# Spectral layer and gated FFN on one core: the first transform stage as four 64x64 quarters, the third stage in halves through one PSUM bank, one instruction for both bias additions

## The chip, the core and the metric

The kernel runs on one core of a Trainium2 chip. The metric is the device time of one execution in microseconds (us). The core has TensorE (PE in the profile, with PEld for its weight loads), VectorE (DVE), ScalarE (ACT), GpSimd (POOL), and SyncE (SP), which here only issues DMAs. TensorE writes into PSUM, eight banks of 2 KB per partition; a bank holds 512 float32 values per partition.

## The reference, cut to what matters

```python
X = np.fft.rfft(x, axis=1)                       # x: 8 x 3136 x 256
Xr, Xi = X.real, X.imag
Yr = Xr @ w_r - Xi @ w_i + b_r                   # 256 x 256 mixing, complex
Yi = Xr @ w_i + Xi @ w_r + b_i
Y = softshrink(Yr, 0.01) + 1j * softshrink(Yi, 0.01)
y = np.fft.irfft(Y, n=3136, axis=1)
h = np.maximum(y @ w_in, 0)                      # 256 -> 1024
gate = sigmoid(conv3_along_seq(h, conv_w))
out = (h * gate) @ w_out                         # 1024 -> 256
```

A complex transform of length 3136 along the sequence, a 256x256 complex mix with bias and soft threshold, the inverse transform, and then a gated feed-forward layer.

## The kernel before, in words

The transform of length 3136 = 56 x 56 is done in two matmul stages each way, and everything up to the inverse's first half is one pipeline over 56 items: 8 batches `b` times 7 groups `g` of four frequencies.

- **Stage 1** (`stage1`, and `stage1_head` for batch 0): a DFT of length 56 over the slow index `n` for a block of four columns `j` (`JC = 4`). Two interleaved sequences (`h` = 0, 1, even and odd `n`) are done together: the weights `f1` are a 112x112 matrix with the 56x56 DFT table in it twice and zeros elsewhere. One block is two float32 matmuls of 112 rows by 512 columns into a single bank (`ps_s1`, one buffer), each followed by an ACT copy into `a1`; one DMA loads the block's `xr` from `x`, one DMA stores `a1` into the DRAM scratch `sc1`.
- **Stage 2** (`stage2`): reads `sc1` back in another layout (`load_a2`) and does the second DFT, eight float32 matmuls of 128 columns. The result is split into a rounded part `fh` and a rest `fl` (ACT and DVE).
- **Mix** (`mix`): 36 matmuls into three banks `ps_mx0..2` (Karatsuba: three real products for a complex one). DVE adds each of the two biases to the third product (`p1`, two instructions, line 309), adds the other two products (line 313, four instructions), then the soft threshold on ACT and DVE, and a split into `sh` and `sl`.
- **Stage 3** (`stage3`): twelve matmuls into two banks `ps_s3` (four outputs of 256 columns), one ACT copy into `z1`, one DMA to the scratch `sc2`.
- After this pipeline, **stage 4** finishes the inverse transform and `up`/`down` do the feed-forward layer (from about 550 us to the end).

In this first part the eight banks are: 1 `ps_s1`, 2 `ps_s2`, 3 `ps_mx`, 2 `ps_s3`.

The main loop over `it` emits stage 2 of item `it`, the mix of item `it-1`, stage 3 of item `it-3`, and one or two stage 1 blocks ahead (`min(it + AHEAD, NG + 2 + it + it // 2)`). A generator `later()` converts the feed-forward weights from 64-bit floats beside it; each `next(background)` is about one DVE instruction of that conversion: five per item early, then 2.2 on average. The code's order is only the start: a list scheduler orders each engine's queue, and `reuse_waits` pools and PSUM buffers set what waits for what. All DMAs are issued by SP in order. The first batch's blocks are loaded at once (`hx0..6`; the first in two DMAs) and go through `stage1_head`, which borrows the `ps_mx` banks and shares the copies between ACT and DVE.

A float32 matmul in this program appears in the trace as two MATMUL records, each with a weight load ahead of it: stage 1's 98 instructions at line 245 are 196 records. They are called passes below. `float32r` matmuls (mix, stage 3, feed-forward) are one record each.

Of the kernel before, what the change touches and what calls it, by code (L numbers as in the profile page):

```python
# [9 lines left out]
F32 = mybir.dt.float32  # L10
# [4 lines left out]
ALU = mybir.AluOpType  # L15
PSUM = bass.MemoryType.PSUM
DRAM = bass.MemoryType.DRAM

B, S, D, FF = 8, 3136, 256, 1024
R = 56  # L20
U = 28
SL = 57
SP = 64
H = 28
LAM = 0.01
UG = 4
NG = U // UG
JC = 4
P = 128
# [5 lines left out]
def _tables():  # L35
    n = np.arange(R)
    u = np.arange(U)

    f = np.zeros((R, 2, U))
# [3 lines left out]
    f[:, 1, 0] = np.where(n % 2 == 0, 1.0, -1.0)  # L43
    fwd1 = np.zeros((2, R, U, 2, 2))
    for h in range(2):
        fwd1[h, :, :, :, h] = f.transpose(0, 2, 1)

# [8 lines left out]
    for uu in range(U):  # L56
        for s in range(SL):
# [14 lines left out]
            elif s < R:  # L72
                k = uu + R * s
# [14 lines left out]
    return {  # L88
        "fwd1": fwd1.transpose(1, 0, 2, 3, 4).reshape(2 * R, 2 * R).astype(np.float32),
        "fwd2": fwd2.reshape(2 * R, U * 2 * SP).astype(np.float32),  # L90
# [6 lines left out]
def spectral_ffn_kernel(ctx: ExitStack, tc: tile.TileContext, x, w_r, w_i, b_r, b_i,  # L97
# [19 lines left out]
    with ExitStack() as ab:  # L117
# [6 lines left out]
        DB, XRB, SL_ENG = 1, 3, nc.gpsimd  # L124
        ps1 = ab.enter_context(tc.tile_pool(name="ps1", bufs=1, space=PSUM))
        ps2 = ab.enter_context(tc.tile_pool(name="ps2", bufs=2, space=PSUM))
        psm = ab.enter_context(tc.tile_pool(name="psm", bufs=1, space=PSUM))
        psa = ab.enter_context(tc.tile_pool(name="psa", bufs=1, space=PSUM))

        f1 = c1.tile([K1, P], F32, name="f1")[:, 0:K1]  # L130
        t2 = c1.tile([K1, U, K2], F32, name="t2")
# [97 lines left out]

        def load_x(pool, b, jc, parts=1, **kw):  # L230

            xr = pool.tile([K1, JC, D], F32, name="xr", **kw)
            xv = x[b].rearrange("(n j) d -> n j d", j=H)[:, jc * JC:(jc + 1) * JC, :]
            w = JC // parts
            for k in range(0, JC, w):
                ld = nc.sync.dma_start(xr[:, k:k + w, :], xv[:, k:k + w, :])
            return xr, ld

        def stage1(b, jc):

            xr, _ = load_x(s1p, b, jc, bufs=XRB)
            a1 = s1p.tile([K1, JC, D], F32, name="a1", bufs=2)
            for j in range(0, JC, 2):
                ps = ps1.tile([K1, 2, D], F32, name="ps_s1")
                nc.tensor.matmul(ps, f1, xr[:, j:j + 2, :], start=True, stop=True)  # L245
                nc.scalar.copy(a1[:, j:j + 2, :], ps)  # L246
            return nc.sync.dma_start(sc1[b][:, jc * JC:(jc + 1) * JC, :], a1)

        def stage1_head(xs, b=0):

            with tc.tile_pool(name="ha", bufs=1, reuse_waits="tile") as ha:
                for jc, xr in enumerate(xs):
                    a1 = ha.tile([K1, JC, D], F32, name=f"ha{jc}")
                    for j in range(0, JC, 2):
                        k = (jc * 2 + j // 2) % 4
                        if k < 3:
                            ps = psm.tile([K1, 2, D], F32, name="ps_s1h", tag=f"ps_mx{k}")
                        else:
                            ps = ps1.tile([K1, 2, D], F32, name="ps_s1")
                        nc.tensor.matmul(ps, f1, xr[:, j:j + 2, :], start=True, stop=True)  # L260
                        if j:
                            nc.vector.tensor_copy(a1[:, j:j + 2, :], ps)
                        else:
                            nc.scalar.copy(a1[:, j:j + 2, :], ps)
                    st = nc.sync.dma_start(sc1[b][:, jc * JC:(jc + 1) * JC, :], a1)
            return st
# [24 lines left out]
        def mix(xs):  # L291
# [15 lines left out]
            half = (slice(0, SP), slice(SP, K2))  # L307
            for c in range(2):
                nc.vector.tensor_tensor(p1[:, c], ps[2], bias[:, c], op=ALU.add)
            for c in range(2):  # L310
# [13 lines left out]
        def stage3(b, g, s):  # L324

            sh, sl, _ = s
            ps = psa.tile([K1, UG, D], F32, name="ps_s3")
            for k in range(UG):
                u = g * UG + k
                for n, (lt, rh) in enumerate(((i1_hi, sh), (i1_hi, sl), (i1_lo, sh))):  # L330
                    nc.tensor.matmul(ps[:, k, :], lt[:, u, :], rh[:, k, :], start=(n == 0), stop=(n == 2))  # L331
            z1 = io.tile([K1, UG, D], F32, name="z1", bufs=2)
            nc.scalar.copy(z1, ps)
            nc.sync.dma_start(sc2[b][:, g * UG:(g + 1) * UG, :], z1)
# [12 lines left out]
        with tc.tile_pool(name="hx", bufs=1, reuse_waits="tile") as hx:  # L347
            xh = []
            for p in range(NG):
                xr, ld = load_x(hx, 0, p, parts=2 if p == 0 else 1, tag=f"hx{p}")  # L350
                xh.append(xr)
            with tc.issue_after(ld.ins):
                load_t2(0)
                load_mix()
                load_bias()
                st = stage1_head(xh)
# [16 lines left out]
        for it in range(n_it + 3):  # L373
# [15 lines left out]
            if WP0 <= it < n_it:  # L389
                with tc.issue_after(ss[it - 1][2].ins):  # L390
                    for _ in range(5 if it < CW_IT else 2 + (it % 5 == 0)):
                        next(background, None)
# [148 lines left out]
```

## Time and profile before

| | |
|---|---|
| median of 3 runs | 1766.77 us (1766.06 to 1769.52) |
| the profiled execution | 1769.05 us, its span 1767.3 us |
| granted TensorE clock | 0.995 |
| PE busy | 1731.0 us (98%), 12096 matmul records |
| PE weight loads | 1621.6 us (92%) |
| DVE busy | 1524.3 us (86%) |
| ACT busy | 1229.1 us (70%) |
| POOL busy | 134.7 us (8%) |
| DMA | 164.63 MB, 30.9% of 16 engines' span |

The profile is of one execution; 1.75 us lie around its span, and it is 2.28 us above the median of the runs. Busy time of PE counts a matmul until its modelled end, and successive matmuls overlap, so the distance between the starts of two matmuls is what one costs, and not its duration. The "chain" is followed back from the last instruction to whatever released each step.

### The profile page before, as it was taken

Reading aid. Unit: us, or ns where it says so; the run is one execution under the profiler, and the core shown is the slowest. Engines: PE = TensorE matmul, PEld = TensorE weight load, DVE = VectorE, ACT = ScalarE, POOL = GpSimd, SP = SyncE. Lnnn points to the kernel's source line nnn. Section 1 sums busy time; section 2 is a strip of 40 time slices with the busy share of each in tenths; the row PEclk is TensorE's granted clock in tenths of the full one; section 3 lists DMA queues with packets and bytes.
Section 4 is the critical chain, followed back from the end, with each engine's and each line's share of the span. In section 5 each row is a group of like instructions: output and inputs, shape, how many; then the busy total and the mean of one; then the engine's idle time right before and its main releaser. Section 6 shows DMA issues by size and latency. Waiting matters only on the chain.

```text
span 1767.3 us, 29387 instructions
## 1 busy us (share of the span) xinstructions
PE 1731.0 (98%) x12096; PEld 1621.6 (92%) x12096; DVE 1524.3 (86%) x1820; ACT 1229.1 (70%) x1590; POOL 134.7 (8%) x60
## 2 busy tenths in 40 slices
PE   6899999999998999999999999999999999999999
PEld 2788888888998999999999999999999999999998
DVE  2899999998896988988888888888888888888887
ACT  2667777776665777777777777777777777777766
POOL 0122222222232000000000000000000000000000
PEclk8999999999999999999999999999999999999999
DMA  9777677677534110111111011111101111100001
GB/s 263 216 230 236 196 232 216 192 230 228 164 111 136 43 43 22 32 53 53 32 53 53 22 55 51 49 46 52 43 22 43 53 43 43 42 22 22 22 22 42
DMA packets 107382, 164.63 MB, mean 93 GB/s; under 512 B 8816, under 2 KB 86000, under 8 KB 107248
## 3 DMA queue, kind: packets, MB, share of 16 engines
q1 hardware_dynamic: 107248, 162.74, 30.9%
q8 instruction: 96, 1.57, 0.4%
q14 instruction: 38, 0.31, 0.1%
HBM read 85.65 MB, written 77.07 MB: 92 GB/s over the span
## 4 chain that ended last, share of the span: by engine, by line
PE 93%; DMA 3%; DVE 1%; ACT 1%; issue 0%; SPq 0%; ACTq 0%
PE acc L470 31%; PE ps_h L442 31%; PE ps_mx L304 12%; PE ps_s L423 5%; PE ps_s L280 5%; PE ps_s L331 4%; PE ps_s L245 4%; DMA i_raw<-in_inv_dram 2%; DMA z<-sc 1%; DMA sc<-ha 0%; DMA a<-sc 0%; DMA sc<-a 0%; ACT a L246 0%; DVE cw L212 0%; DVE yl L430 0%
## 5 line engine op out<-in xcount | busy, mean ns | idle before, releaser
L470 PE MATMUL acc<-wout,gh 128*128 128x256 f32 x3136 | 567.0, 280 | 0.0
L451 DVE SCALAR_TENSOR_TENSOR c<-h,cw,c 128x896 f32<-128x896 f32 x448 | 513.1, 1147 | 47.3 <-ACT c L449 46.3
L442 PE MATMUL ps_h<-yh,win 128*128 128x450 f32 x1792 | 551.0, 368 | 0.1
L470 PEld LDWEIGHTS acc<-wout,gh 128*128 128x128 f32 x3136 | 493.7, 188 | 6.5
L470 PE MATMUL acc<-wout,gl 128*128 128x256 f32 x1568 | 437.6, 281 | 0.0
L444 ACT ACTIVATE h<-ps_h 128x900 f32<-128x900 f32 x224 | 207.7, 927 | 254.8 <-PE ps_h L442 254.8
L442 PEld LDWEIGHTS ps_h<-yh,win 128*128 128x128 f32 x1792 | 338.7, 189 | 26.4 <-DVE yl L430 0.8
L442 PE MATMUL ps_h<-yl,win 128*128 128x450 f32 x896 | 329.2, 367 | 0.0
L470 PEld LDWEIGHTS acc<-wout,gl 128*128 128x128 f32 x1568 | 293.7, 188 | 0.1
L457 DVE TENSOR_TENSOR gl<-c,gh 128x896 fp32r<-128x896 f32 x224 | 243.1, 1089 | 53.6 <-ACT gh L456 50.1
L453 DVE TENSOR_TENSOR c<-h,c 128x896 f32<-128x896 f32 x224 | 243.6, 1088 | 46.9 <-ACT c L452 46.7
L456 ACT CAST gh<-c 128x896 fp32r<-128x896 f32 x224 | 209.8, 942 | 49.4 <-DVE c L453 49.4
L452 ACT ACTIVATE c<-c 128x896 f32<-128x896 f32 x224 | 213.3, 952 | 23.9 <-DVE c L451 21.0
L304 PE MATMUL ps_mx<-wmix_lo,fh 128*128 128x256 f32 x672 | 202.2, 301 | 0.0
L304 PE MATMUL ps_mx<-wmix_hi,fh 128*128 128x256 f32 x672 | 196.9, 294 | 0.5 <-DVE v L313 0.3
L304 PE MATMUL ps_mx<-wmix_hi,fl 128*128 128x256 f32 x672 | 188.7, 282 | 1.3 <-DVE fl L288 1.2
L442 PEld LDWEIGHTS ps_h<-yl,win 128*128 128x128 f32 x896 | 168.9, 189 | 11.0
L449 ACT ACTIVATE c<-h,cw 128x896 f32<-128x896 f32 x168 | 175.5, 1044 | 2.6 <-DVE gl L457 0.2
L321 POOL TENSOR_TENSOR sl<-v,sh 128x1024 fp32r<-128x1024 f32 x56 | 134.5, 2402 | 423.1 <-PE ps_s L331 300.0
L313 DVE TENSOR_TENSOR v<-ps_mx,p 64x512 f32<-64x512 f32 x224 | 154.0, 688 | 3.3
L304 PEld LDWEIGHTS ps_mx<-wmix_lo,fh 128*128 128x128 f32 x672 | 126.4, 188 | 12.3 <-issue 12.3
L304 PEld LDWEIGHTS ps_mx<-wmix_hi,fl 128*128 128x128 f32 x672 | 126.0, 188 | 11.8 <-issue 9.9
(84 smaller groups left out, 2023.0 us busy)
## 6 DMA issues: line engine op xcount, KB each, us to landing
a<-sc SPq DMA_DIRECT2D x56, 448.0 KB, 5.0
sc<-z SPq DMA_DIRECT2D x56, 448.0 KB, 3.3
z<-sc SPq DMA_DIRECT2D x56, 448.0 KB, 3.8
xr<-in_x_dram SPq DMA_DIRECT2D x55, 448.0 KB, 4.7
out_dram<-o SPq DMA_DIRECT2D x27, 896.0 KB, 4.0
sc<-a SPq DMA_DIRECT2D x49, 448.0 KB, 4.9
sc<-ha SPq DMA_DIRECT2D x7, 448.0 KB, 7.5
win_bits<-in_moe_w_in_dram SPq DMA_DIRECT2D x4, 512.0 KB, 7.6
```

What stands on the lines that cost most here:

```text
L304: nc.tensor.matmul(ps[c][:, k, :], lt, rh, start=(n == 0), stop=(n == len(mm) - 1))
L313: nc.vector.tensor_tensor(v[dst, :, k, :], ps[c][src], p1[src, c], op=ALU.add)
L321: SL_ENG.tensor_tensor(sl, v, sh.bitcast(F32), op=ALU.subtract)
L442: nc.tensor.matmul(ps[:, a, 0:CH + 2], lt, rh, start=(n == 0), stop=(n == len(mm) - 1))
L444: nc.scalar.activation(h, ps[:, :, 0:CH + 2], AF.Relu)
L449: nc.scalar.mul(c, h[:, :, 0:CH], cw[:, 0, f:f + 1])
L451: nc.vector.scalar_tensor_tensor(c, h[:, :, k:k + CH], cw[:, k, f:f + 1], c, op0=ALU.mult, op1=ALU.add)
L452: nc.scalar.activation(c, c, AF.Sigmoid)
L453: nc.vector.tensor_tensor(c, h[:, :, 1:CH + 1], c, op=ALU.mult)
L456: nc.scalar.copy(gh, c)
L457: nc.vector.tensor_tensor(gl, c, gh.bitcast(F32), op=ALU.subtract)
L470: nc.tensor.matmul(acc[m // 2][:, m % 2, :], lt[:, sl], rh[:, f, :], start=(f == 0 and n == 0 and m % 2 == 0), stop=(f == NF - 1 and n == ...
```

## The change

- `fwd1` becomes one 56x56 table, padded to 64x64 and placed twice, at partitions 0 and 64. `xr` has the even `n` on partitions 0 to 55 and the odd on 64 to 119, loaded by two DMAs.
- `quarters` does a block in four matmuls of 56 rows and 64 output columns, with 512 moving columns each: for each pair of columns `c` and each `h`, rows `h*64..`, output partitions `c*64..`, bank `ps[h]`. In the program these four carry an array tile of 64x64 at the four positions (0,0), (0,64), (64,0), (64,64).
- `ps1` has two buffers, one bank for each `h`. The ACT copies stay two of 512 columns, now on 128 partitions; the store is two DMAs, with runs of 2 KB where there were 4 KB.
- To free the bank, stage 3 uses one bank and goes in two halves, six matmuls and an ACT copy each.
- The bias sums `p1` are one DVE instruction of 1024 columns that reads the PSUM bank twice, where there were two of 512.
- The weight conversion beside the loop goes at 1.67 steps per item after the early ones, where it went at 2.2.
- The head's first block is not loaded by columns in two parts any more, and its copies and banks alternate by block.

```diff
...
-    fwd1 = np.zeros((2, R, U, 2, 2))
-    for h in range(2):
-        fwd1[h, :, :, :, h] = f.transpose(0, 2, 1)
+    fwd1 = np.zeros((2, SP, SP))
+    fwd1[:, :R, :R] = f.transpose(0, 2, 1).reshape(R, R)
...
-        ps1 = ab.enter_context(tc.tile_pool(name="ps1", bufs=1, space=PSUM))
+        ps1 = ab.enter_context(tc.tile_pool(name="ps1", bufs=2, space=PSUM))
...
-        f1 = c1.tile([K1, P], F32, name="f1")[:, 0:K1]
+        f1 = c1.tile([P, P], F32, name="f1")[:, 0:SP]
...
+            xr = pool.tile([P, JC, D], F32, name="xr", **kw)
+            xv = x[b].rearrange("(n h j) d -> h n j d", h=2, j=H)
+            for h in range(2):
+                ld = nc.sync.dma_start(xr[h * SP:h * SP + R], xv[h, :, jc * JC:(jc + 1) * JC, :])
...
+        def quarters(ps, xr):
+
+            for c in range(2):
+                for h in range(2):
+                    rows = slice(h * SP, h * SP + R)
+                    nc.tensor.matmul(ps[h][c * SP:(c + 1) * SP], f1[rows, :], xr[rows, 2 * c:2 * c + 2, :], start=True, stop=True)
+
+        def store_a1(b, jc, a1):
+
+            for c in range(2):
+                j = jc * JC + 2 * c
+                st = nc.sync.dma_start(sc1[b].rearrange("(w h) j d -> w h j d", h=2)[:, :, j:j + 2, :], a1[c * SP:c * SP + R])
+            return st
+
         def stage1(b, jc):
 
             xr, _ = load_x(s1p, b, jc, bufs=XRB)
-            a1 = s1p.tile([K1, JC, D], F32, name="a1", bufs=2)
-            for j in range(0, JC, 2):
-                ps = ps1.tile([K1, 2, D], F32, name="ps_s1")
-                nc.tensor.matmul(ps, f1, xr[:, j:j + 2, :], start=True, stop=True)
-                nc.scalar.copy(a1[:, j:j + 2, :], ps)
-            return nc.sync.dma_start(sc1[b][:, jc * JC:(jc + 1) * JC, :], a1)
+            a1 = s1p.tile([P, 2, JC // 2, D], F32, name="a1", bufs=2)
+            ps = [ps1.tile([P, JC // 2, D], F32, name="ps_s1") for h in range(2)]
+            quarters(ps, xr)
+            for h in range(2):
+                nc.scalar.copy(a1[:, h], ps[h])
+            return store_a1(b, jc, a1)
...
-            for c in range(2):
-                nc.vector.tensor_tensor(p1[:, c], ps[2], bias[:, c], op=ALU.add)
+            nc.vector.tensor_tensor(p1, ps[2].unsqueeze(1).broadcast_to([K2, 2, UG // 2, D]), bias, op=ALU.add)
...
-            ps = psa.tile([K1, UG, D], F32, name="ps_s3")
-            for k in range(UG):
-                u = g * UG + k
-                for n, (lt, rh) in enumerate(((i1_hi, sh), (i1_hi, sl), (i1_lo, sh))):
-                    nc.tensor.matmul(ps[:, k, :], lt[:, u, :], rh[:, k, :], start=(n == 0), stop=(n == 2))
             z1 = io.tile([K1, UG, D], F32, name="z1", bufs=2)
-            nc.scalar.copy(z1, ps)
+            for c in range(0, UG, 2):
+                ps = psa.tile([K1, 2, D], F32, name="ps_s3")
+                for k in range(2):
+                    u = g * UG + c + k
+                    for n, (lt, rh) in enumerate(((i1_hi, sh), (i1_hi, sl), (i1_lo, sh))):
+                        nc.tensor.matmul(ps[:, k, :], lt[:, u, :], rh[:, c + k, :], start=(n == 0), stop=(n == 2))
+                nc.scalar.copy(z1[:, c:c + 2, :], ps)
...
-                    for _ in range(5 if it < CW_IT else 2 + (it % 5 == 0)):
+                    for _ in range(5 if it < CW_IT else 1 + (it % 3 > 0)):
...
```

The scheduler also moves instructions. On TensorE, this is a round in the middle of the pipeline before, word for word from the program's order (`ps_s` with a number is a PSUM tile: line 331 writes stage 3's, 245 stage 1's, 280 stage 2's):

```order
L331 MATMUL ps_s_1382<-sl,i_hi 112x256
L331 MATMUL ps_s_1382<-sh,i_lo 112x256
L245 MATMUL ps_s_1401<-xr,f_113 112x512
L280 MATMUL ps_s_1420<-t_114,a_1195 128x128 x4
L280 MATMUL ps_s_1429<-t_114,a_1195 128x128 x4
L304 MATMUL ps_mx_1442<-wmix_hi,fh 128x256
...
L245 MATMUL ps_s_1404<-xr,f_113 112x512
```

Each stage 1 matmul stands alone between others, twice a round, and stage 3's twelve are together. The same part of a round of the changed program (line 242 is `quarters`, 340 stage 3, 288 stage 2, 312 the mix):

```order
L340 MATMUL ps_s_2252<-sh,i_lo 112x256
L312 MATMUL ps_mx_2313<-wmix_hi,fl 128x256
L242 MATMUL ps_s_2723<-xr,f_113 64x512
L312 MATMUL ps_mx_2311<-wmix_hi,fh 128x256
...
L340 MATMUL ps_s_2260<-sh,i_hi 112x256
...
L288 MATMUL ps_s_2402<-t_114,a_2173 128x128 x4
L288 MATMUL ps_s_2411<-t_114,a_2173 128x128 x4
L312 MATMUL ps_mx_2424<-wmix_hi,fh 128x256
L312 MATMUL ps_mx_2424<-wmix_lo,fh 128x256
L242 MATMUL ps_s_2724<-xr,f_113 64x512
L242 MATMUL ps_s_2723<-xr,f_113 64x512
L242 MATMUL ps_s_2724<-xr,f_113 64x512
```

The four quarters of a block (tiles 2723 and 2724, two each) are put apart: one, then 26 mix and six stage 3 matmuls and stage 2's eight, then three. Stage 3's second half (2260) stands 20 mix matmuls and a quarter behind the first (2252). Counted over the whole order, the 224 quarters lie in 84 runs with no other matmul inside: one run of 34 at the start, then 14 runs of four, 12 of three, 41 of two, 16 of one. Up to the fourth mix there are 52 quarters in 9 runs (before: 24 matmuls), from there 172 quarters in 75 runs (before: 88 matmuls). The last quarter stands after the 36th of 56 mixes, where the last stage 1 matmul before stood after the 46th.

On SP, the DMAs of a round before (line 334 stores `z1`, 270 loads `a2`, 236 loads `xr`, 247 stores `a1`):

```order
L334 DMA sc_1_66<-z_1940 112x1024
L270 DMA a_2065<-sc_2_59 112x4x256
L236 DMA xr<-in_x_dram 112x1024
L247 DMA sc_3_60<-a_1945 112x1024
L334 DMA sc_1_66<-z_2049 112x1024
```

and of one in the changed program (342, 278, 234, 248 in the same order):

```order
L342 DMA sc_2_67<-z_2588 112x1024
L234 DMA xr<-in_x_dram 56x1024 x2
L248 DMA sc_4_61<-a_3172 112x1x512 x2
L278 DMA a_2962<-sc_3_60 112x4x256
L342 DMA sc_2_67<-z_2701 112x1024
```

The loads of `xr` and the stores of `a1` are two issues each, of half the size; the order of the kinds is the same but for `a2`.

More of the change, by code (lines that the diff above doesn't have):

```diff
@@ L88, in _tables @@
     return {
-        "fwd1": fwd1.transpose(1, 0, 2, 3, 4).reshape(2 * R, 2 * R).astype(np.float32),
+        "fwd1": fwd1.reshape(2 * SP, SP).astype(np.float32),
         "fwd2": fwd2.reshape(2 * R, U * 2 * SP).astype(np.float32),
@@ L228, in later, with load_x @@
                     yield from split_weight(*asked.pop(0))
[L230 to L236, printed above, removed]
-            return xr, ld
+        def load_x(pool, b, jc, **kw):
+            xr = pool.tile([P, JC, D], F32, name="xr", **kw)
+            xv = x[b].rearrange("(n h j) d -> h n j d", h=2, j=H)
+            for h in range(2):
+                ld = nc.sync.dma_start(xr[h * SP:h * SP + R], xv[h, :, jc * JC:(jc + 1) * JC, :])
+            return xr, ld
+        def quarters(ps, xr):
[8 more added lines that the diff above has]
+            return st
         def stage1(b, jc):
             xr, _ = load_x(s1p, b, jc, bufs=XRB)
-            a1 = s1p.tile([K1, JC, D], F32, name="a1", bufs=2)
-            for j in range(0, JC, 2):
-                ps = ps1.tile([K1, 2, D], F32, name="ps_s1")
-                nc.tensor.matmul(ps, f1, xr[:, j:j + 2, :], start=True, stop=True)
-                nc.scalar.copy(a1[:, j:j + 2, :], ps)
-            return nc.sync.dma_start(sc1[b][:, jc * JC:(jc + 1) * JC, :], a1)
+            a1 = s1p.tile([P, 2, JC // 2, D], F32, name="a1", bufs=2)
[4 more added lines that the diff above has]
+            return store_a1(b, jc, a1)
         def stage1_head(xs, b=0):
@@ L252, in stage1_head @@
                 for jc, xr in enumerate(xs):
[L253 to L265, printed above, removed]
+                    a1 = ha.tile([P, 2, JC // 2, D], F32, name=f"ha{jc}")
+                    if jc % 2:
+                        ps = [psm.tile([P, JC // 2, D], F32, name="ps_s1h", tag=f"ps_mx{h}") for h in range(2)]
+                    else:
+                        ps = [ps1.tile([P, JC // 2, D], F32, name="ps_s1") for h in range(2)]
+                    quarters(ps, xr)
+                    nc.scalar.copy(a1[:, 0], ps[0])
+                    nc.vector.tensor_copy(a1[:, 1], ps[1])
+                    st = store_a1(b, jc, a1)
             return st
@@ L349, in spectral_ffn_kernel @@
             for p in range(NG):
-                xr, ld = load_x(hx, 0, p, parts=2 if p == 0 else 1, tag=f"hx{p}")
+                xr, ld = load_x(hx, 0, p, tag=f"hx{p}")
                 xh.append(xr)
```

## The prediction

> **What bounds the kernel now.** First the chain of waits on the page, then the busy time by windows, to find the stretch in which the changed stages run and what limits it.
>
> ```profile
> PE 93%; DMA 3%; DVE 1%; ACT 1%; issue 0%; SPq 0%; ACTq 0%
> ```
>
> ```profile
> core 0: us, PE busy (x) PEld busy (x) DVE busy (x) ACT busy (x) POOL busy (x), PEclk, DMA share, GB/s
> 0.00:25.00 25.00, 16.95 (x28) 5.87 (x28) 7.94 (x14) 7.04 (x12) 0.20 (x4) 1.00 0.90 264
> 25.00:50.00 25.00, 15.60 (x80) 11.88 (x81) 7.64 (x14) 7.67 (x16) 0.00 (x0) 0.73 0.97 238
> 50.00:75.00 25.00, 20.18 (x143) 17.13 (x143) 20.99 (x34) 13.70 (x24) 2.41 (x1) 1.00 0.93 261
> 75.00:100.00 25.00, 23.61 (x172) 20.55 (x170) 23.12 (x40) 16.70 (x31) 7.48 (x3) 1.00 0.52 150
> 100.00:120.00 20.00, 18.90 (x132) 16.04 (x133) 17.66 (x36) 13.69 (x23) 4.75 (x2) 1.00 0.90 265
> 160.00:250.00 90.00, 90.00 (x671) 80.09 (x670) 85.04 (x138) 65.42 (x104) 23.81 (x10) 1.00 0.77 227
> 480.00:550.00 70.00, 66.48 (x566) 65.87 (x565) 67.39 (x109) 47.20 (x69) 22.84 (x10) 0.99 0.38 112
> 600.00:1767.00 1167.00, 1162.96 (x7989) 1119.93 (x7988) 1011.57 (x1004) 836.14 (x977) 0.00 (x0) 1.00 0.13 40
> ```
>
> Up to 120 us PE is busy for 16.95 + 15.60 + 20.18 + 23.61 + 18.90 = 95.2 us of 120: 24.8 us of idle PE lie there, beside DMA engines at 0.90 to 0.97 in most of it. From 160 us PE never stops (90.00 of 90.00), while DVE has 85.04 and ACT 65.42 of the same 90. Behind 550 us the feed-forward layer runs, which the change doesn't touch. So what stage 1 costs is what it takes of PE, in the stretch in which PE is full.
>
> What one instruction costs on PE is read from the distance between starts, in the chain and in the timeline.
>
> ```profile
> 109.52 0.86 PE ps_s L245 x2
> 155.55 3.04 PE ps_mx L304 x26
> 164.69 3.04 PE ps_mx L304 x26
> ```
>
> ```profile
> 150.60 0.28 PE L331 MATMUL ps_s<-sh,i_lo 128*112 128x256 f32 x1
> 150.72 1.02 PE L245 MATMUL ps_s<-xr,f 112*112 112x512 f32 x2
> 151.58 1.95 PE L280 MATMUL ps_s<-t,a 112*128 112x128 f32 x16
> ```
>
> One stage 1 matmul holds PE for 0.86 us (150.72 to 151.58), as two records: a pass of 512 columns costs 0.43 us. A mix matmul costs 3.04 / 26 = 0.117 us. A round of the pipeline lasts 164.69 - 155.55 = 9.14 us, and its two stage 1 matmuls are 1.72 us of it.
>
> ```profile
> L245 PE MATMUL ps_s<-xr,f x196: 590/592/1167, 32.6 to 474.7; 112*112 112x512 f32 x196
> ```
>
> A pass's record lasts 0.592 us at the median, 0.16 us beyond the 0.43 after which the next one starts: results are still on their way out of the array while the next matmul already runs.
>
> **The change part by part.** *Quarters.* A block had two matmuls of two passes, 4 x 0.43 = 1.72 us. Now it has four matmuls of two passes each over 512 columns; nothing in the diff makes a pass shorter, since the columns that stream through are as many. So it is eight passes, and all depends on how many run at the same time on different quarters of the array, which no record of this kernel shows: every matmul here uses the full array. The bounds are 8 x 0.43 = 3.44 us (none at a time) and 0.86 us (all four).
>
> I take a value between, from the order. The timeline shows PE's matmuls starting in program order, and a quarter's second pass uses the same rows of the array as its first, so it can't start until the first has streamed, 0.43 us later. The next quarter stands behind that second pass. In an in-order queue its first pass can start beside it, but not earlier. So n quarters in a row take (n + 1) passes: a block in one piece 5 x 0.43 = 2.15 us, and in two pieces of two 6 x 0.43 = 2.58. Both are more than 1.72. The Trainium skill, TensorE: Matmul & The Clock Gate, "The mechanism", says that tiles of the array overlap, but that matmuls start and end strictly in the order of the program; the timeline agrees on the starts, and no run here shows tiles.
>
> From the fourth mix on, about where PE is full, the order has 172 quarters in 75 runs in place of 88 matmuls: (172 + 75) x 0.43 = 106.2 us in place of 88 x 0.86 = 75.7. That is **+30.5 us**.
>
> *Going in and out of quarters.* Each run begins and ends beside full-array matmuls. If the array must be empty before it is divided in another way, the 0.16 us by which records overlap is lost at each border: 75 x 2 x 0.16 = **+24.0 us**. The bounds are 0 (matmuls of different shapes, 112 and 128 rows, follow each other without a gap now) and 0.34 us a border, if the weight load of the next matmul isn't hidden either:
>
> ```profile
> L245 PEld LDWEIGHTS ps_s<-xr,f 112*112 112x112 f32 x196 | 29.0, 178 | 18.4 <-issue 11.4 <-ACT a L246 7.0
> L246 ACT COPY a<-ps_s 112x512 f32<-112x512 f32 x98 | 58.3, 595 | 19.7 <-PE ps_s L245 18.4 <-DMA sc<-a 0.4
> L333 ACT COPY z<-ps_s 112x1024 f32<-112x1024 f32 x56 | 56.7, 1013 | 78.8 <-PE ps_s L331 74.7 <-DMA sc<-a 4.0
> L309 DVE TENSOR_TENSOR p<-ps_mx,bias 128x512 f32<-128x512 f32 x112 | 71.8, 684 | 0.2
> L319 DVE SCALAR_TENSOR_TENSOR v<-v,r 128x1024 f32<-128x1024 f32 x56 | 70.1, 1251 | 16.7 <-ACT r L318 16.2
> ```
>
> (0.16 + 0.178 = 0.34, so up to 51 us). I take 0.16, since the load is hidden by the matmul ahead wherever PE is full now. The Trainium skill, TensorEngine Tiling (Array Packing), "Key Properties", has this rule: a change of the tiling mode, not of the tile alone, drains TensorE. It speaks against the change; the trace has no such border.
>
> *Up to the fourth mix* there are 52 quarters in 9 runs for 24 matmuls: 61 x 0.43 = 26.2 us for 20.6, and 18 borders x 0.16 = 2.9, so 8.5 us more of PE, beside 24.8 us of idle PE. Most of it is hidden by transfers that end later; I take **+2 us** (0 to 8.5).
>
> *Stage 3 in halves.* Two ACT copies of 512 columns (595 ns by line 246) for one of 1024 (1013 ns) are 0.18 us more of ACT in a round, where ACT has (90 - 65.42) / 90 x 9.14 = 2.5 us free: nothing. The new wait is that of the second half's first matmul for the copy of the first half; behind it on PE stand the mix matmuls, and for these DVE waits. In the order 20 mix matmuls lie between, 2.3 us, and ACT stood idle for 74.7 us in 56 rounds waiting for just this stage, so it takes the copy at once: 0. If a copy of 1.0 us (line 333's length) is ahead of it and only twelve mix matmuls (1.4 us) lie between, the wait is 1.0 + 0.6 - 1.4 = 0.2 us a round, 11 us in all: the other bound.
>
> *Bias in one instruction.* A DVE instruction of 1024 columns takes 1251 ns (line 319) and two of 512 take 1368: 0.12 us less of DVE a round. DVE isn't what the round waits for (85.04 of 90): 0. The same for the slower weight conversion, which only spreads DVE work over more rounds.
>
> *DMAs and SP.* Two issues more for each load and each store; on SP the next issues behind them are `z1` and `a2`.
>
> ```profile
> xr<-in_x_dram SPq DMA_DIRECT2D x55, 448.0 KB, 4.7
> sc<-a SPq DMA_DIRECT2D x49, 448.0 KB, 4.9
> ```
>
> They land within 5 us now, and a block is loaded rounds ahead: nothing in the full stretch, where the DMA share is 0.77. In the first 75 us shorter runs may cost or spare a microsecond or two: -2 to +3, I take 0.
>
> Sum: 30.5 + 24.0 + 2 = +56.5 us. The profiled execution took 1769.05 us, 2.28 above the median: 1825.5 there, **1823 us** as a median.
>
> **The rivals.**
>
> *No overlap at all*, so that the quarters do not do what their tiles say: 172 x 0.86 = 147.9 for 75.7 us, +72.2, with the borders +24.0, and the first run of 34 quarters (29.2 us for about 14.6 before) delays the first stores by some 8 us: +104, 1871 us. For it: nothing in the trace shows two matmuls side by side. Against it: the instructions have disjoint rows or columns and disjoint banks.
>
> *Full overlap within a run*, if each quarter has a queue of its own, so that the next quarter needn't wait for the second pass ahead. A run then takes 0.86 us whatever its length: 75 x 0.86 = 64.5 for 75.7, which is -11.2. With borders of 0.16 us it ends at -11.2 + 24.0 = +13, 1780 us. What limits the gain is in the order: only 14 runs hold four quarters, and a run of one or two costs as much.
>
> *Full overlap and free borders*, which is the other side: -11.2 us, about 1756 us. It decides as soon as a border costs less than 11.2 / 150 = 0.075 us. A round would then be shorter at the cost of DVE's slack, and DVE, at 85.04 / 90 x 9.14 = 8.6 us a round less the 0.12 of the bias, would be next; the rounds with quarters, (75 x 0.86) / 32 + 7.4 = 9.4 us (7.4 = 9.14 - 1.72; 32 rounds from the fourth mix to the 36th), stay above that, so DVE takes nothing back. For it: full-array matmuls of unlike shapes border without a gap today. Against it: a second pass would have to be overtaken. The Trainium skill, TensorEngine Tiling (Array Packing), "Key Properties", has tiles loading weights and multiplying in parallel, independently of each other; on that rule alone, this case would be the likeliest.
>
> **How the numbers follow.** The forecast with (n + 1) passes has 0.42; its own range goes from free borders (1769.05 - 2.28 + 30.5 = 1797) to borders of 0.34 us (1850). No overlap has 0.20, full overlap with borders 0.20, full overlap and free borders 0.18. A measurement of this kernel tells 0.2%, 3.5 us, from no change. Faster is the last case and a little of the one before it with small borders, 0.20; within 0.2% is only a border cost near 0.075 us, 0.06; slower the rest, 0.74. The range goes from 1754 to 1855: it holds all cases but no overlap.
>
> **What would show it.** In the profile after, the distance between the starts of line 242's records inside a run of four: eight records over five distances of 0.43 us if I am right, over two if all overlap, over eight if none do. At a border: the distance from the last quarter's start to the next full-array matmul, 0.43 us if it is free and 0.59 if the array empties. PE should stay full from 120 to about 500 us, with rounds of about 11.4 us ((106.2 + 24.0) / 32 + 7.4) up to the 36th mix and of 7.4 behind it, and line 340 should not wait for ACT. A round of 9.4 us or less, DVE as the engine waited for, or DMA waits at line 242 would prove me wrong.

## The result, and the profile after

The changed kernel takes **1832.38 us** (median of 4 runs, 1830.94 to 1834.84) beside 1768.14 us of the kernel before on the same chip (4 runs, 1766.06 to 1773.74): a ratio of **1.0353, 95% interval 1.0337 to 1.0369**. It is slower by 64 us. Its profiled execution took 1833.43 us, with a span of 1831.2.

First the chain of waits on the page of the changed kernel, by engine. Before, it read PE 93%, DMA 3%, DVE 1%.

```profile
PE 79%; DVE 13%; issue 4%; DMA 2%; ACT 1%; SPq 1%; POOL 0%; DVEq 0%; ACTq 0%
```

Then its busy time by windows, the stretches of before where they can be compared.

```profile
core 0: us, PE busy (x) PEld busy (x) DVE busy (x) ACT busy (x) POOL busy (x), PEclk, DMA share, GB/s
0.00:25.00 25.00, 12.98 (x44) 3.19 (x44) 4.66 (x9) 5.38 (x9) 0.21 (x4) 1.00 0.81 206
...
160.00:250.00 90.00, 85.66 (x623) 67.20 (x622) 78.09 (x104) 55.71 (x100) 21.84 (x9) 1.00 0.69 205
...
480.00:550.00 70.00, 63.07 (x521) 60.88 (x520) 69.20 (x104) 45.89 (x79) 19.71 (x8) 1.00 0.46 126
```

From 160 to 250 us PE was busy for 90.00 of 90; now it has 4.3 us of gaps, and DVE is less busy as well (78.09 for 85.04). Neither engine is full: they wait for each other. Within the pipeline, the chain by line (here from 120 to 500 us) goes through PE for less than half.

```profile
by line: PE ps_mx L312 21.0%; PE ps_s L242 11.6%; issue 11.2%; DVE v L320 8.2%; PE ps_s L288 7.4%; PE ps_s L340 7.1%; DVE fl L294 6.3%; DVE p L316 5.7%; DVE fl L296 4.4%; DVE v L326 2.4%; DVE d L293 2.4%; POOL sl L328 1.3%; DVE win_m L198 1
```

**Where the 64 us lie.** The start of the soft threshold on DVE (line 326; 319 before) marks each of the 56 items. Read off the timelines of the two profiled executions:

| start of the soft threshold of | item 4 | item 40 | item 55 |
|---|---|---|---|
| before | 98.6 us | 427.6 us | 550.2 us |
| after | 109.2 us | 492.5 us | 614.2 us |
| lost up to there | 10.6 | 64.9 | 64.0 |

So 10.6 us are lost in the head, 54.3 in the 36 rounds from item 4 to item 40 (383.3 / 36 = 10.65 us a round, for 329.0 / 36 = 9.14), and nothing behind them. The last quarter runs at 436.7 us; some 5 of the 54.3 us are lost behind it, between items 36 and 40 (59.6 us lost up to item 36).

**The quarters overlap.** This is PE's timeline of the changed kernel around a run of three quarters, with the mix matmuls on both sides.

```profile
213.12 0.28 PE L312 MATMUL ps_mx<-wmix_hi,fl 128*128 128x256 f32 x1
213.34 1.08 PE L242 MATMUL ps_s<-xr,f 56*64 56x512 f32 x6
214.35 0.38 PE L312 MATMUL ps_mx<-wmix_hi,fh 128*128 128x256 f32 x1
214.57 0.28 PE L312 MATMUL ps_mx<-wmix_lo,fh 128*128 128x256 f32 x1
```

Six passes that would take 6 x 0.43 = 2.6 us one behind another hold PE for 1.01 us (213.34 to 214.35). Shorter stretches of the same timeline part the six records: three start together, and three start together 0.47 us later.

```profile
213.34 0.65 PE L242 MATMUL ps_s<-xr,f 56*64 56x512 f32 x3
...
213.81 0.60 PE L242 MATMUL ps_s<-xr,f 56*64 56x512 f32 x3
```

The first passes of neighbours start 7 ns apart, and only then come the second passes. Runs of one, two, three and four quarters hold PE for 1.00, 1.01, 1.01 and 1.02 us at the median. The distances on both sides are stretched too: 0.22 us instead of 0.12 from the last mix matmul to the first quarter, and 0.22 from the first to the second mix matmul behind. From the last mix matmul ahead to the second behind it is 1.45 us, less two usual distances of 0.117: **a run costs 1.21 us**, whatever its length, where one full-array matmul cost 0.86. The border, in and out, is 0.35 us a run.

The Trainium skill, TensorEngine Tiling (Array Packing), "Key Properties", states that tiles work in parallel and that a change of mode drains TensorE; the trace agrees with the first. The longer distances on both sides fit the second, and 0.35 us is the price of two changes here; but the ends of matmuls are modelled, so the trace doesn't show whether the array is empty at a border.

**But PE is not all that the rounds wait for.** From item 4 to item 40 the idle time between PE's records grows from 2.1 to 18.6 us. Here is a run of four in the same kernel, 6 us earlier, and what comes behind it.

```profile
206.88 0.28 PE L312 MATMUL ps_mx<-wmix_lo,fh 128*128 128x256 f32 x1
207.08 1.09 PE L242 MATMUL ps_s<-xr,f 56*64 56x512 f32 x8
209.82 0.39 PE L312 MATMUL ps_mx<-wmix_hi,fl 128*128 128x256 f32 x1 [1.65 <-DVE fl L296]
```

PE stands still for 1.65 us behind the quarters, until DVE has written `fl`. DVE's and GpSimd's timeline of that moment:

```profile
205.18 1.21 DVE L326 SCALAR_TENSOR_TENSOR v<-v,r 128x1024 f32<-128x1024 f32 x1
206.32 2.85 DVE L198 TENSOR_TENSOR win_m<-win_m,win 128x512 f32<-128x512 f32 x1
209.09 0.68 DVE L296 TENSOR_TENSOR fl<-d,fh 128x512 fp32r<-128x512 f32 x1
209.69 0.68 DVE L199 TENSOR_TENSOR win<-win_m,win_rest 128x512 fp32r<-128x512 f32 x1
...
205.63 2.98 POOL L328 TENSOR_TENSOR sl<-v,sh 128x1024 fp32r<-128x1024 f32 x1 [7.96 <-PE ps_s L340]
```

Line 198 and line 199 are the same kind of instruction on tiles of the same size, and yet 2.85 us and 0.68. The long one lies under GpSimd's split `sl` (line 328, 205.63 to 208.61) and ends 0.56 us behind it (9.17 - 8.61): it did not run slowly, it waited. Behind it in DVE's order stands line 296, and for that PE waits. The same moment before:

```profile
204.18 0.69 DVE L199 TENSOR_TENSOR win_m<-win_m,win 128x512 f32<-128x512 f32 x1
204.78 0.69 DVE L288 TENSOR_TENSOR fl<-d,fh 128x512 fp32r<-128x512 f32 x1
205.39 2.81 DVE L313 TENSOR_TENSOR v<-ps_mx,p 64x512 f32<-64x512 f32 x4
...
205.73 2.37 POOL L321 TENSOR_TENSOR sl<-v,sh 128x1024 fp32r<-128x1024 f32 x1 [6.76 <-PE ps_s L331]
```

Here the split (205.73 to 208.10) lies under the four additions of line 313 (205.39 to 208.20), which read one operand from PSUM, and none of the four is longer for it (2.81 / 4 = 0.70 us). The line views of the changed kernel say the same over all items. Min, median and max in ns:

```profile
L320 DVE TENSOR_TENSOR v<-ps_mx,p x224: 667/689/696, 65.1 to 612.3; 64x512 f32<-64x512 f32 x112
...
L296 DVE TENSOR_TENSOR fl<-d,fh x56: 676/683/2872, 52.9 to 600.2; 128x512 fp32r<-128x512 f32 x56
```

Line 320 reads PSUM and never exceeds 696 ns, line 296 reads two tiles in SBUF and reaches 2872. Between 40 and 620 us of the timeline, DVE instructions that stand by themselves and are longer than 1.3 us number 5 before (5.5 us beyond their usual length) and **25 after (47 us)**, and all of the 25 lie under the split. The Trainium skill, SBUF — State Buffer, "SBUF: two separate sides", states that VectorE and GpSimd share a pair of SBUF ports as an exclusive lock, held for a whole instruction, which a VectorE instruction with two SBUF inputs takes too; the trace agrees, for the two kinds of instruction above.

What moved the split is in the waits. It writes `sl`, which has one buffer, so it waits until stage 3 of the item ahead has read the old `sl`. Of the kernel after, from 120 to 500 us: engine and line, what it waited for, us in total, times, longest:

```profile
POOL sl L328 <- PE ps_s L340: 270.5, 34, 10.5
DVE v L320 <- POOL sl L328: 34.3, 14, 3.2
ACT d L291 <- DVE fl L296: 22.2, 13, 2.9
```

The wait for stage 3 was there before, in the same window:

```profile
POOL sl L321 <- PE ps_s L331: 267.1, 40, 7.6
```

But stage 3 now ends later: its second half stands 20 mix matmuls and a quarter behind the first, as the order showed, and in the traces it starts 5.3 us behind it at the median of items 4 to 40, where it was 0.7. From the end of `sh` to the start of the split the median of these items went from 2.8 us to 8.8, out from under the PSUM additions. Since `v` has to live until the split has read it, line 320 now waits for GpSimd too: 34.3 us.

**The head.** SP's queue, first the kernel after and then before:

```profile
1.19 9.48 SPq L234 DMA_DIRECT2D xr<-in_x_dram  x14
...
13.61 0.39 SPq L152 DMA_DIRECT2D wm_raw<-in_w_i_dram  x1
...
19.48 14.14 SPq L248 DMA_DIRECT2D sc<-ha  x14
...
36.91 1.40 SPq L278 DMA_DIRECT2D a<-sc  x3
```

```profile
1.18 4.32 SPq L236 DMA_DIRECT2D xr<-in_x_dram  x8
...
8.42 0.38 SPq L153 DMA_DIRECT2D wm_raw<-in_w_i_dram  x1
...
16.80 7.76 SPq L265 DMA_DIRECT2D sc<-ha  x7
...
30.72 1.39 SPq L270 DMA_DIRECT2D a<-sc  x3
```

The first load of stage 2's input is issued 6.2 us later. All of DVE's copies of the head but the first stand behind the split of the mix weights (line 156) in its order, and that waits for the `w_i` load, issued 5.2 us later. Before, four of them ran ahead of that split, from 7.98 to 16.98 us.

```profile
9.97 0.69 DVE L272 COPY ha<-ps_s1h 128x512 f32<-128x512 f32 x1 [1.90 <-PE ps_s1h L242]
21.33 0.69 DVE L156 TENSOR_TENSOR wm<-wm_raw,wm_raw 128x512 f32<-128x512 f32 x1 [10.67 <-DMA wm_raw<-in_w_i_dram]
...
22.55 0.68 DVE L272 COPY ha<-ps_s 128x512 f32<-128x512 f32 x1
```

### The profile page after: what moved, and what is told of

Same layout as the page of the kernel before. It is cut to its first block, busy times and chain, and to the rows that moved or that the text cites. A ratio compares the mean times of both kernels' runs of the same rounds, so it can differ in the third digit from the quotient of the medians.

```text
span 1831.2 us, 29833 instructions
## 1 busy us (share of the span) xinstructions
PE 1767.7 (97%) x12320; PEld 1617.2 (88%) x12320; DVE 1561.4 (85%) x1764; ACT 1231.8 (67%) x1646; POOL 143.8 (8%) x60
## 4 chain that ended last, share of the span: by engine, by line
PE 79%; DVE 13%; issue 4%; DMA 2%; ACT 1%; SPq 1%; POOL 0%; DVEq 0%; ACTq 0%
PE ps_h L450 30%; PE acc L478 30%; PE ps_mx L312 6%; PE ps_s L431 5%; DVE v L320 3%; PE ps_s L242 3%; PE ps_s L288 3%; PE ps_s L340 2%; DVE fl L294 2%; DVE p L316 2%; DMA xr<-in_x_dram 1%; DVE fl L296 1%; DVE v L326 1%; DVE d L293 1%; DMA wm_raw<-in_w_i_dram 0%
## 5 line engine op out<-in xcount | busy, mean ns | idle before, releaser
L312 PE MATMUL ps_mx<-wmix_lo,fh 128*128 128x256 f32 x672 | 189.7, 282 | 0.0
L320 DVE TENSOR_TENSOR v<-ps_mx,p 64x512 f32<-64x512 f32 x224 | 153.9, 687 | 37.5 <-POOL sl L328 34.3
L328 POOL TENSOR_TENSOR sl<-v,sh 128x1024 fp32r<-128x1024 f32 x56 | 143.6, 2565 | 483.8 <-PE ps_s L340 316.3
L312 PEld LDWEIGHTS ps_mx<-wmix_hi,fh 128*128 128x128 f32 x672 | 128.8, 192 | 28.4 <-DVE v L320 7.5
```

The lines of the kernel that those rows point to most:

```text
L312: nc.tensor.matmul(ps[c][:, k, :], lt, rh, start=(n == 0), stop=(n == len(mm) - 1))
L320: nc.vector.tensor_tensor(v[dst, :, k, :], ps[c][src], p1[src, c], op=ALU.add)
L328: SL_ENG.tensor_tensor(sl, v, sh.bitcast(F32), op=ALU.subtract)
```

## The experiments

**Theory 1**: stage 3 in halves makes `sl` live longer; GpSimd's split starts later and falls on DVE instructions that read only SBUF, and these, with PE behind them, are the lost rounds. **Theory 2**: the rounds are lost to the quarters themselves, scattered in runs with a border each, and to what they made of the order. All ratios are to the kernel before, run on the same chip; medians of 4 or 5 runs.

| | ratio, 95% interval | item 4 | rounds 4 to 40 | long DVE instr. |
|---|---|---|---|---|
| before | 1 | 98.6 us | 9.14 us | 5 |
| after | 1.0353 (1.0337 to 1.0369) | 109.2 | 10.65 | 25 |
| split on VectorE | 1.0274 (1.0256 to 1.0291) | 110.6 | 9.93 | 0 |
| before + halves | 1.0262 (1.0247 to 1.0278) | 100.8 | 10.28 | 48 |
| after, `sl` in two tiles | 1.0110 (1.0093 to 1.0127) | 105.7 | 9.33 | 17 |
| after, two `sl` buffers | 1.0182 (1.0166 to 1.0197) | 108.9 | 9.47 | 20 |
| before + quarters | 1.0212 (1.0196 to 1.0229) | 105.5 | 9.91 | 6 |
| before + halves, `sl` in two tiles | 1.0038 (1.0024 to 1.0052) | 96.3 | 9.35 | 17 |

### The split on VectorE (e1)

```diff
-        DB, XRB, SL_ENG = 1, 3, nc.gpsimd
+        DB, XRB, SL_ENG = 1, 3, nc.vector
```

> The changed kernel, with the split sl = v - sh on VectorE in place of GpSimd. Theory 1 (what costs the time is GpSimd's split: 25 VectorE instructions that overlap it take 47 us more than usual, and line 320 waits 34 us for it): no VectorE instruction above 1.3 us is left, VectorE has 1.1 us more of its own in a round, and the time falls to 1775 to 1805 us. Theory 2 (the quarters put in 84 places and the new order cost the time, on TensorE): VectorE only gets more to do, 1835 to 1890 us.

1816.72 us. With nothing on GpSimd not one DVE instruction is longer than usual, and the kernel is 16 us faster than the change although DVE has 56 x 1.22 = 68 us more to do. But the time lies between the ranges of both theories. Its windows, DVE being the third pair of numbers:

```profile
160.00:250.00 90.00, 90.00 (x673) 72.06 (x672) 86.02 (x125) 60.84 (x109) 0.00 (x0) 1.00 0.74 225
...
430.00:480.00 50.00, 46.49 (x361) 43.12 (x359) 49.33 (x72) 31.01 (x53) 0.00 (x0) 0.97 0.40 123
```

The run shows that the long instructions need GpSimd at work. It also shows that they are not all of the loss: with PE full from 160 to 250 us, the 36 rounds still take 357.6 us, 28.6 more than before. Later DVE, which now does the split, is full (49.33 of 50 us), and items 40 to 55 take 136.1 us where they took 121.8 in the change.

### The halves alone (e2)

The kernel before, with stage 3 as in the change and one bank for it; stage 1 untouched.

```diff
-            ps = psa.tile([K1, UG, D], F32, name="ps_s3")
...
-            nc.scalar.copy(z1, ps)
+            for c in range(0, UG, 2):
+                ps = psa.tile([K1, 2, D], F32, name="ps_s3")
...
+                nc.scalar.copy(z1[:, c:c + 2, :], ps)
```

> The kernel before, with nothing changed but stage 3 in halves through one bank (one bank is left empty). Theory 1 (halves release the one sl buffer later, so that GpSimd's split starts later and meets VectorE instructions that read only SBUF): slower than before by 15 to 60 us, with VectorE instructions of 2.8 us in the trace. Theory 2 (the quarters are the cause): within 5 us of the kernel before.

1814.67 us: **+46 us without a single quarter**. The timeline, a DVE instruction ahead, then one under the split:

```profile
245.35 0.69 DVE L188 SCALAR_TENSOR_TENSOR win_e<-win_bits,win_e 128x512 int32<-128x512 int32 x1
245.95 2.60 DVE L189 TENSOR_SCALAR win_m<-win_bits 128x512 int32<-128x512 int32 x1
...
245.47 2.79 POOL L321 TENSOR_TENSOR sl<-v,sh 128x1024 fp32r<-128x1024 f32 x1 [8.29 <-PE ps_s L333]
```

GpSimd waits 8.29 us for stage 3, and then the two engines exclude each other. From 160 to 250 us DVE looks full:

```profile
160.00:250.00 90.00, 83.51 (x603) 72.70 (x602) 89.20 (x125) 57.77 (x102) 23.07 (x9) 1.00 0.68 201
```

But 48 of its instructions hold some 66 us of waiting: a busy time can hold a wait. From item 4 to item 40, 512 instructions keep DVE busy for 360.9 of 369.9 us, where 507 took 308.6 of 329.0 before. So DVE's time grew by 52 us for the same work, in rounds that grew by 41. Theory 2 has no place for this run.

### `sl` in two tiles, `sl` with two buffers (e3, e4)

```diff
-            sl = wk.tile([K2, UG, D], F32R, name="sl", bufs=1)
+            sl = [wk.tile([K2, 2, D], F32R, name=f"sl{c}", bufs=1) for c in range(2)]
...
-            SL_ENG.tensor_tensor(sl, v, sh.bitcast(F32), op=ALU.subtract)
+            for c in range(2):
+                SL_ENG.tensor_tensor(sl[c], v[:, 2 * c:2 * c + 2], sh[:, 2 * c:2 * c + 2].bitcast(F32), op=ALU.subtract)
```

> The changed kernel, with sl as two tiles of two outputs each, and GpSimd's split as two instructions of 512 columns: each half can start when that half of stage 3 is done with its tile. Theory 1: the split starts earlier, collisions are half as long, 1785 to 1815 us. Theory 2: 1828 to 1838 us, as the changed kernel.

```diff
-            sl = wk.tile([K2, UG, D], F32R, name="sl", bufs=1)
+            sl = wk.tile([K2, UG, D], F32R, name="sl", bufs=2)
```

> The changed kernel, with two sl buffers, so that GpSimd's split waits only for sh and no more for stage 3. Theory 1: the split moves to another place in the round; the wait of line 320 for GpSimd (34 us) goes, and what is left of the 47 us depends on which VectorE instructions lie there: 1775 to 1815 us. Theory 2: 1828 to 1838 us.

1786.29 and 1801.23 us, both in the range of theory 1, with rounds of 9.33 and 9.47 us. With two tiles the first half of the split is free as soon as stage 3's first half is through, and a collision costs 1.1 us at most (17 long instructions, 14 us). With two buffers the wait for stage 3 is gone, and the split follows `sh` at once (0.1 us at the median). In the waits of that kernel, from 120 to 500 us, the cast is now what it waits for:

```profile
POOL sl L328 <- ACT sh L327: 265.6, 37, 11.7
```

It still meets SBUF-only instructions there (20 long ones, 21 us). A reservation on both: their orders have 56 runs of quarters (41 of four) where the change has 84, and the second half of stage 3 starts 3.4 us behind the first, where it was 5.3. At 1.21 us a run, 28 runs fewer are 34 us less of PE. So neither run parts the collisions from the quarters. The next one has no quarters.

### The halves with `sl` in two tiles (e11)

The kernel before with both edits, the halves of e2 and the two tiles of e3; no quarters.

> The kernel before with stage 3 in halves through one bank and sl in two tiles, no quarters. It parts the two readings of the run with two sl tiles, whose order also had fewer runs of quarters (56 in place of 84). Theory 1: the 46 us of the halves alone go mostly, 1768 to 1785 us. Theory 2 for that run (its gain was that of the fewer runs): 1805 to 1820 us, as the halves alone.

1777.55 us: the 46 us of the halves are down to 7. Nothing in the code differs from e2 but the grain of `sl`, so **39 of the 46 us hang on the grain of `sl`, and neither the single bank nor the two copies cost them**. The order of the queues changed with it: the second half of stage 3 starts 3.6 us behind the first at the median, and 5.2 in e2. So the run doesn't part the split's length from the place that the new order gives it. DVE's busy time from item 4 to item 40 speaks for the collisions: 323.7 us, of 360.9 in e2. PE is full again, or nearly:

```profile
160.00:250.00 90.00, 89.26 (x668) 79.64 (x667) 88.27 (x138) 64.34 (x114) 25.60 (x20) 1.00 0.75 225
```

and each GpSimd instruction (1.28 us) waits half as long as before:

```profile
205.81 1.28 POOL L322 TENSOR_TENSOR sl<-v,sh 128x512 fp32r<-128x512 f32 x1 [3.88 <-ACT sh L320]
...
209.03 1.27 POOL L322 TENSOR_TENSOR sl<-v,sh 128x512 fp32r<-128x512 f32 x1 [1.94 <-PE ps_s L334]
```

### The quarters alone (e5)

The kernel before with stage 1 in 64x64 quarters, stage 3 whole in its two banks. With only one bank left for stage 1, a block goes in two runs of two (one for each `h`), never four.

```diff
+        def quarters(ps, xr, h):
+
+            for c in range(2):
+                rows = slice(h * SP, h * SP + R)
+                nc.tensor.matmul(ps[c * SP:(c + 1) * SP], f1[rows, :], xr[rows, 2 * c:2 * c + 2, :], start=True, stop=True)
...
+            for h in range(2):
+                ps = ps1.tile([P, JC // 2, D], F32, name="ps_s1")
+                quarters(ps, xr, h)
+                nc.scalar.copy(a1[:, h], ps)
```

> The kernel before with the quarters, but without the halves: the two column quarters of one h go into the single ps_s1 bank, then those of the other h, and stage 3 stays whole in two banks (bias additions and pace as before). Its order has 97 runs, 96 of them pairs. Theory 1 (halves and GpSimd's split cost most of it): the split stays where it was, no more VectorE instructions above 1.3 us than before (5), and the time is that of before plus about 88 x 0.23 = 20 us for pairs of 1.09 us in place of matmuls of 0.86, and up to 10 us in the head: 1785 to 1800 us. Theory 2 (quarters scattered over the order are the cause): 1815 us or more.

1808.43 us, over the range of theory 1 and under that of theory 2: I had put the border at 0.23 us, from the record's tails. A run in this kernel:

```profile
203.31 0.28 PE L342 MATMUL ps_s<-sh,i_lo 128*112 128x256 f32 x1
203.52 1.07 PE L241 MATMUL ps_s<-xr,f 56*64 56x512 f32 x4
204.53 1.72 PE L291 MATMUL ps_s<-t,a 112*128 112x128 f32 x13
```

0.21 us ahead of it where full-array matmuls follow each other in 0.12, and 1.01 us to the next: with 0.35 us for a border and 88 runs in place of 88 matmuls that is 31 us, and 7 more stand at item 4. Together 38, as measured. Here PE is the bound, as the prediction had it for the whole change:

```profile
160.00:250.00 90.00, 90.00 (x663) 72.86 (x662) 81.34 (x129) 62.12 (x98) 21.37 (x9) 1.00 0.67 199
```

and there are 6 long DVE instructions, as few as before: the quarters bring none. The costs of the two parts, 46 and 38, don't add up to the 64 of the change. They fall in the same rounds; as far as PE waits for DVE there, a border costs nothing, which is argued from the rounds and not measured by itself.

So each theory has a part. Of the 54.3 us that the change loses from item 4 to item 40, 28.6 are left when GpSimd does nothing (e1), and the quarters alone cost 27.7 there (e5); 0.35 us for each of the 71 to 73 runs of quarters between these marks is 25. The other 26 us go with GpSimd's split. The shares are an estimate, since e1's order differs from that of the change.

### The head's DMAs on two queues (e6, e7)

One of each pair of head loads and stores is issued on ACT's queue instead of SP's, on the change (e6) and on the change with `sl` in two tiles (e7).

```diff
-                ld = nc.sync.dma_start(xr[h * SP:h * SP + R], xv[h, :, jc * JC:(jc + 1) * JC, :])
+                ld = (other, nc.sync)[h].dma_start(xr[h * SP:h * SP + R], xv[h, :, jc * JC:(jc + 1) * JC, :])
```

> The changed kernel, with one of the two DMAs of each head load and each head store issued by ACT's queue in place of SP's; TensorE's order is the same. If the head's loss of 11 us (item 0's threshold at 71.2 us in place of 60.0) comes from SP issuing 28 DMAs where it issued 15: item 0 at 60 to 66 us and the whole 5 to 10 us faster, 1822 to 1828 us. If it comes from transfers or from TensorE: no change, 1830 to 1835 us.

> The two-tile sl together with the head's DMAs on two queues. If both losses are what they were said to be they add up: 1786 less 5 to 10, 1776 to 1781 us. If the pipeline behind takes the head's gain back: 1784 to 1788 us.

1830.96 us (1.0331, 1.0314 to 1.0349) and 1786.18 us (1.0086, 1.0069 to 1.0102): neither can be told from its kernel without the edit. Item 4 starts at 106.6 us instead of 109.2 in e6, and at 106.8 instead of 105.7 in e7. So fewer issues on SP do not speed up the head. Whether SP's time is what holds it back is not decided, because the edit hardly shortened it. SP's queue in e6:

```profile
1.20 9.17 SPq L234 DMA_DIRECT2D xr<-in_x_dram  x7
...
14.43 0.39 SPq L152 DMA_DIRECT2D wm_raw<-in_w_i_dram  x1
```

Its seven loads take as long to issue as the fourteen of the change (9.48 us), and the `w_i` load goes out at 14.43 us, no earlier than at 13.61.

### Bias and pace undone (e8)

The change, with two bias instructions again and the conversion's old pace.

```diff
-            nc.vector.tensor_tensor(p1, ps[2].unsqueeze(1).broadcast_to([K2, 2, UG // 2, D]), bias, op=ALU.add)
+            for c in range(2):
+                nc.vector.tensor_tensor(p1[:, c], ps[2], bias[:, c], op=ALU.add)
...
-                    for _ in range(5 if it < CW_IT else 1 + (it % 3 > 0)):
+                    for _ in range(5 if it < CW_IT else 2 + (it % 5 == 0)):
```

> The changed kernel with two instructions for the bias additions again and the pace of the weight conversion as before (2.2 steps an item). If these two parts do little, as the prediction has it: 1825 to 1842 us (its order has 72 runs of quarters in place of 84). If they are a cause of the loss, by moving VectorE's instructions against GpSimd's split: 1800 us or less.

1826.57 us (1.0320, 1.0306 to 1.0334), with 32 long instructions and 72 runs of quarters for the 84 of the change. The two small edits together gain nothing here; undone, the kernel is 0.3% faster, and the two intervals just part.

### Whole blocks of four, and the old head (e9, e12, e13)

Could the quarters pay, once the collisions are halved? On e7, the two banks become one tile, so that a block's four quarters are one wait and its copy is one instruction of 1024 columns: 44 of 53 runs are then fours (e9). Then the first batch is done again in full-array matmuls with a table of its own, loads and stores on SP alone (e12), and the conversion goes slower still (e13).

```diff
-            ps = [ps1.tile([P, JC // 2, D], F32, name="ps_s1") for h in range(2)]
-            quarters(ps, xr)
-            for h in range(2):
-                nc.scalar.copy(a1[:, h], ps[h])
+            ps = ps1.tile([P, 2, JC // 2, D], F32, name="ps_s1")
+            quarters([ps[:, h] for h in range(2)], xr)
+            nc.scalar.copy(a1, ps)
```

> The changed kernel with sl in two tiles, the head's DMAs on two queues, and ps_s1 as one tile of two banks with one copy of 1024 columns, so that a block's four quarters become free to run together: 53 runs in the order, 44 of them of four. A run holds TensorE for 1.21 us whatever its length, so against the run with two sl tiles (56 runs) it changes little on TensorE; ACT has 0.18 us less a round: 1775 to 1786 us.

> The same as the one before, with the first batch done as in the kernel before (full-array matmuls with their own table, one DMA a load and a store, all on SP). If the head's loss of 10 us belongs to the head's own form: item 0's threshold at 60 us, and 8 to 11 us faster than the run with the new head: 1764 to 1776 us. If the pipeline behind takes it back: no change.

```diff
-                    for _ in range(5 if it < CW_IT else 1 + (it % 3 > 0)):
+                    for _ in range(5 if it < CW_IT else 1 + (it % 2)):
```

> The same with the weight conversion at 1.5 steps an item (1 or 2 in turn) in place of 1.67. VectorE has 0.1 us less in a round up to the 36th: if VectorE sets the round there, 2 to 6 us faster than the run with the old head; else the same within 2 us.

1787.77 us (1.0095, 1.0079 to 1.0110), 1780.30 (1.0063, 1.0051 to 1.0076) and 1783.90 (1.0074, 1.0062 to 1.0087). e9 and e12 came out above their ranges, and e13 is 3.6 us slower than e12 where it was to be faster or the same (the intervals overlap): I had priced the longer runs by PE, and PE isn't what these kernels wait for. The chain of e12 from 150 to 400 us:

```profile
by line: DVE v L337 25.5%; issue 11.5%; DVE p L333 10.0%; DVE fl L311 9.8%; PE ps_mx L329 8.0%; ACT r L342 6.0%; DVE fl L313 5.6%; DVE v L343 4.7%; DVE d L310 4.2%; PE ps_s L305 2.7%; PE ps_s L358 2.2%; PE ps_s L247 2.1%; DVE wout_m L194 0.
```

DVE's own additions (line 337) lead it; PE has 86.12 and DVE 85.37 of 90 us. What the runs of four spare on PE is not on the path. With the old head item 4 starts at 102.5 us (e12) and 96.8 (e13), for 108.2 in e9. The runs e12 and e13 have the same order up to there, so one execution's figure for item 4 is uncertain by some 5 us. Over all runs the new head and the old one part: 105.5 to 110.6 us in the nine kernels with the new one, 96.3 to 102.5 in the five with the old, some 8.6 us between the means. None of these kernels beats the one before.

## Why the prediction was right or wrong

The number held, 1823 forecast and 1832 measured, and so did the sign; but two steps under it were wrong, and their errors nearly cancelled: some 42 us too much for the quarters, and nothing for halves that cost 46 us by themselves.

- **"n quarters in a row take (n + 1) passes"** failed. All quarters of a run go at once: two passes for any n. The term was not +30.5 us but 75 x 0.86 - 75.7 = -11.2, as the rival of full overlap had it. The failing argument was that the next quarter stands behind the second pass ahead of it; in the trace all first passes come ahead of all second ones. Whether the program holds them in that order or PE passes them is not shown.
- **"0.16 us at each border", +24.0**, was right in kind and nearly in size: 0.35 us for the two borders of a run, where 0.32 was taken. With both, PE has 75 x 1.21 - 75.7 = +15 us, close to the second rival's +13.
- **"Stage 3 in halves: 0, bounded by 11"** failed worst: it costs 46 us alone. The step looked at one wait, that of the second half's matmuls for ACT, and this wait is as small as it said: PE stands idle ahead of line 340 for `z1`'s copy four times, 3.6 us in all. It did not follow the buffer. The second half reads `sl`, the split of the next item waits for the last such read, and the split's place in time decides which DVE instructions it shuts out. The trace of before had this wait as GpSimd's longest (267.1 us), and GpSimd's 8% of busy time made it look free. That GpSimd's instruction holds DVE up is shown; how much of the 46 us is the split's length and how much the order that came with it stays open (e11).
- **"Full stretch, rounds of 11.4 us, PE full"**: PE is not full, and the rounds take 10.65 us. By the estimate at e5 about half of what they lose is PE's, at the borders, and half DVE's and GpSimd's. The prediction named DVE as the engine waited for as what would prove it wrong, and the chain goes through DVE for some 30% of the time from 120 to 500 us.
- **"Up to the fourth mix +2"**, with 8.5 as its bound, is 10.6. The quarters' head issues and copies later, and over all runs the new form costs some 8.6 us at item 4. Fewer issues on SP did not give it back (e6), but SP's queue was hardly shorter there. Which part of the new form it is (the half loads, the copies' order behind the weight split, the split stores) stays open.
- **Bias and pace, 0**: right within 0.3% (e8, whose order has other runs of quarters). **DMAs and SP in the full stretch, 0**: from 120 to 500 us one kind of wait for a DMA stands out, that of stage 1's ACT copy for the stores of `a1`, four times and 8.3 us in all; the 195 longest pieces of the chain there name no DMA.

That the sum of two wrong terms met the measurement is luck; the rival with the right mechanism on PE gave 1780 and would have been 52 us off, for want of the term for the halves.

## What to carry to other kernels

When a stage is cut into pieces to free a PSUM bank, list every buffer that its last piece reads, and ask who waits to overwrite it and what that will then run beside. Here a GpSimd instruction was free beside DVE instructions that read PSUM and held up those that read only SBUF, so its start mattered more than its share of busy time; cut such an instruction, and its tile, as finely as the stage that reads it. The four array tiles overlapped fully here, but two changes of mode cost 0.35 us, so group tiles in as few and as long runs as the banks allow, and count the borders before counting the overlap.

## What the runs showed of the hardware

- The quarters of a float32 matmul, two passes each, run side by side in both passes: a run of one to four holds PE for 1.00 to 1.02 us, against 0.86 for one full-array matmul of the same columns. The Trainium skill, TensorE: Matmul & The Clock Gate, "The mechanism", has matmuls start strictly in the order of the program; this trace agrees only if the passes are ordered as first passes and then second ones.
- Two changes of the array's mode cost 0.35 us a run, of which about 0.10 lies ahead of the run, 0.10 behind its first successor, and the rest in the run.
- DVE and GpSimd exclude each other in both directions: a 0.69 us DVE instruction took 2.85 under the split, and the split took 2.98 us instead of 2.37 where a DVE instruction with two SBUF inputs (line 326) was ahead of it. DVE instructions with one SBUF input and no PSUM operand are held up too (line 189 in e2, 2.60 us); those with a PSUM operand are not (line 320, at most 696 ns; in none of the kernels here does one exceed its line's shortest by a fifth, between 40 and 620 us).
